# RWKV attention and two expert layers: x2 loads on ScalarE's queue, norm steps placed anew, norm transfers a step later, decay comparison beside the tables

## The chip, the cores and the metric

The kernel runs on one core of a Trainium2 chip. The metric is the device time of one execution in microseconds. Engines are called TensorE (PE in the rows), VectorE (DVE), ScalarE (ACT), GpSimd (POOL) and SyncE (SP, which here only issues transfers).

## The reference, cut to what matters

```python
# attention: B, H, S, D = 4, 8, 768, 48
for t in range(S):
    cur = einsum('bhd,bhe->bhde', u * k[t], v[t])
    y[t] = einsum('bhd,bhde->bhe', r[t], state + cur)
    state = w * state + einsum('bhd,bhe->bhde', k[t], v[t])
# first expert layer: 3072 tokens, 384 -> 768 -> 384
h = maximum(maximum(x @ w1, x @ w2), x @ w3);  x = h @ w_out
# second expert layer: 384 -> 1536 -> 384
xn = x / sqrt(mean(x * x) + 1e-6) * rms_g
g = xn @ w_gate;  val = xn @ w_val
out = (g * sigmoid(g) * val) @ w_out
```

All arrays are float32.

## The kernel before

**Order.** The whole body is one stream written by hand: each engine executes its instructions in the order in which the Python code emits them, and so do the transfer queues of SP and of GpSimd. An instruction that waits holds back all that its engine was given after it. Semaphores are put in by the framework from reads and writes of tiles; a tile of a pool with `bufs=n` takes the place of the tile n before it with the same tag and waits until that one has been read.

**Attention.** Tokens are cut into 24 chunks of 128 (six positions by four batches). `tables()` builds powers of the decay `w` (clamped to 0.7 to 1.1 in `wcl`) by repeated products on VectorE. `decay_flag()` compares `w` with its clamped value (`ok`), sums the comparison with a one-column matmul (`psok`) and makes an integer of it (`nok`); a slow path at the end of the program runs if a decay was clamped. The matmul's bank comes from the pool `psx`, four banks in turn, shared with `pa` (scores), `py` (outputs) and `pkv` (states).

**Units.** The list `UNITS` groups chunks: two of two chunks, five of four. In unit u the main loop runs 18 slots `a_l1` of the first expert layer (f = 0..5, w = 0..2; nine matmuls each into a bank of `psm`, four banks in turn; w = 0 is copied by ScalarE, w = 1, 2 are joined by VectorE's maximum) and, but in the first unit, six slots `a_out`. Between slots, in places set by `LEAD`, it puts the attention steps of the next unit. The flag is taken in unit 1 after slot 8. Products are made of three matmuls on high and low halves (`mm3`, lines 73 to 76), for which ScalarE makes the high half and VectorE or GpSimd subtracts for the low half.

**The last unit** (u = L) has no attention left. After its slot 0 it issues the loads of the first two x2 tiles (output of the first expert layer, kept in DRAM), then the loads of the second expert's weights (`ws_raw`, tiles `gv`, and `wo_raw`, tiles `wof`), all through SP. Between its slots two generators are advanced: `es` (`norm_steps(0)`, then `form_steps(0)`) and `wg` (splitting of weights into high and low halves on ScalarE and GpSimd). The step count of `es` per slot is line 700.

**Norm steps** (lines 546 to 596) for a pair p of x2 tiles, with a yield as a border between steps: 1 to 6 square on ScalarE and add on GpSimd; 7 to 9 and 10 to 12 cast, subtract and sum over partitions with a matmul by ones (`ss`), each closed by a small write to DRAM (`msd`); then a load that spreads the means over partitions (`m`), two idle steps; step 16 the inverse root's start value and two Newton rounds on VectorE, step 17 two more rounds, the write of the roots (`rsd`) and two broadcast loads into `sq`; three idle steps; 21 to 26 scale x2 (line 593). **Form steps** (lines 606 to 631) make four sums and differences, then nine splits; the last three splits wait for slot 18 because they take the place of the unit's own input.

**Second expert.** For each of three pairs p it runs 12 slices f; in each, products `pa`, `pb`, `pc`, `pd`, `px` of the formed inputs with the slice's weights, then the output matmuls. `back(n)`, four times in a slice, advances the weight work (`split_steps`, in pair 0: two splits, then the loads for later slices through SP) and, from slice 2 on, one step of the next pair's norm.

Of the kernel before, what the change touches and what calls it, by code (L numbers as in the profile page):

```python
# [9 lines left out]
F32 = mybir.dt.float32  # L10
# [4 lines left out]
ALU = mybir.AluOpType  # L15
# [22 lines left out]
NP = H // 2  # L38
# [9 lines left out]
def rwkv_moe_kernel(ctx, tc, rkT, rkv, wd, ub, cst, rg, w1p, wo1p, w2p, out):  # L48
    nc = tc.nc
    act, dve, pool, pe, sync = nc.scalar, nc.vector, nc.gpsimd, nc.tensor, nc.sync  # L50
# [8 lines left out]
    tp = sT.enter_context(tc.tile_pool(name="att", bufs=1, side="right"))  # L59
# [121 lines left out]
    qk = tp.tile([96, 2, NP, 128], F32, name="qk")  # L181
    kt = tp.tile([128, DM], F32, name="kt")
    w128 = tp.tile([96, NP], F32, name="w128")
    Tst = [tp.tile([96, NP, 96], F32, name=f"T{b}") for b in range(B)]

    raw_t, tm_t, loads = {}, {}, []
# [16 lines left out]
    def tables():  # L203
        p = ap_.tile([96, NP, 65], F32, tag="h1h", name="ptab")
        pool.memset(p[:, :, 0:1], 1.0)
        dve.tensor_scalar(out=wcl, in0=wsb, scalar1=0.7, scalar2=1.1, op0=ALU.max, op1=ALU.min)
        dve.tensor_copy(p[:, :, 1:2], wcl.unsqueeze(2))
        n = 1
        while n < 64:
            dve.tensor_tensor(out=p[:, :, n + 1:2 * n + 1], in0=p[:, :, 1:n + 1],  # L210
                              in1=p[:, :, n:n + 1].to_broadcast([96, NP, n]), op=ALU.mult)
            n *= 2
        dve.reciprocal(qk[:, 1, :, 64:128], p[:, :, 1:65])
        act.copy(qk[:, 0, :, 64:128], p[:, :, 0:64])
        act.copy(qk[:, 1, :, 0:64], p[:, :, 63::-1])
        act.copy(qk[:, 0, :, 0:64], qk[:, 1, :, 127:63:-1])
        return p
# [13 lines left out]

    def decay_flag():

        ok = tp.tile([96, NP], F32, name="ok")
        dve.tensor_tensor(out=ok, in0=wsb, in1=wcl, op=ALU.is_equal)
        ps = psx.tile([1, NP], F32, tag="x", name="psok")
        pe.matmul(ps, r32(ones[0:96, 0:1]), ok, start=True, stop=True)
        n = cp.tile([1, 1], F32, name="nok")
        dve.tensor_reduce(out=n, in_=ps, op=ALU.add, axis=mybir.AxisListType.X)
        flag = cp.tile([1, 1], mybir.dt.int32, name="okflag")  # L240
        dve.tensor_copy(flag, n)
        return flag
# [219 lines left out]
    with tc.manual_schedule():  # L462
# [83 lines left out]
        def norm_steps(p):  # L546

            br = sB["r"]
            us = (2 * p, 2 * p + 1)
            x = [x2s.pop(u) for u in us]  # L550
            sq = [br.tile([128, 3, 512], F32, tag="sq", bufs=2, name=f"sq{u}") for u in us]
            for j in range(2):
                for k in range(3):
                    act.activation(sq[j][:, k], x[j][:, k], AF.Square)  # L554
                    if k:
                        pool.tensor_tensor(out=sq[j][:, 0], in0=sq[j][:, 0], in1=sq[j][:, k], op=ALU.add)  # L556
                    yield
            for j in range(2):
                sr = br.tile([128, 2, 512], F32R, tag="sr", name=f"sr{us[j]}")
                act.copy(sr[:, 0], sq[j][:, 0])  # L560
                yield
                dve.tensor_tensor(out=sr[:, 1], in0=sq[j][:, 0], in1=r32(sr[:, 0]), op=ALU.subtract)
                yield
                ps = psx.tile([128, 512], F32, tag="x", name=f"ss{us[j]}") if p == 0 else PX[3]
                pe.matmul(ps, ones, sr[:, 0], start=True, stop=False)
                pe.matmul(ps, ones, sr[:, 1], start=False, stop=True)
                act.copy(sq[j][0:1, 1], ps[0:1])
                sync.dma_start(msd[p, j:j + 1], sq[j][0:1, 1])
                yield

            m, y, t = (br.tile([128, 8], F32, tag=f"n{n}", name=f"n{n}{p}") for n in range(3))
            sync.dma_start(m, msd[p].rearrange("j (a b) -> (j a) b", b=8))
            for _ in range(3):
                yield
            dve.tensor_scalar(out=m, in0=m, scalar1=1.0 / DM, scalar2=1e-6, op0=ALU.mult, op1=ALU.add)
            dve.tensor_scalar(out=y.bitcast(U32), in0=m.bitcast(U32), scalar1=1, scalar2=0x7fffffff,
                              op0=ALU.logical_shift_right, op1=ALU.bitwise_xor)
            dve.tensor_scalar(out=y, in0=y, scalar1=1.8352577e-20, scalar2=None, op0=ALU.mult)
            dve.tensor_scalar(out=m, in0=m, scalar1=-0.5, scalar2=None, op0=ALU.mult)
            for n in range(4):  # L580
                if n == 2:
                    yield
                dve.tensor_tensor(out=t, in0=y, in1=m, op=ALU.mult)
                dve.tensor_tensor(out=t, in0=t, in1=y, op=ALU.mult)
                dve.scalar_tensor_tensor(out=y, in0=t, scalar=1.5, in1=y, op0=ALU.add, op1=ALU.mult)
            sync.dma_start(rsd[p].rearrange("j (a b) -> (j a) b", b=8), y)
            for j in range(2):
                sync.dma_start(sq[j][:, 2], rsd[p, j].partition_broadcast(128))
            for _ in range(4):
                yield  # L590
            for j in range(2):
                for k in range(3):
                    dve.scalar_tensor_tensor(out=x[j][:, k], in0=x[j][:, k], scalar=rg_sb[:, k:k + 1],
                                             in1=sq[j][:, 2], op0=ALU.mult, op1=ALU.mult)
                    yield
                xr[us[j]] = x[j]

        def x2_load(u):
            x2s[u] = sB["r"].tile([128, 3, 512], F32, tag="x2", bufs=2, name=f"x2_{u}")
            sync.dma_start(x2s[u], x2d[u])  # L600

        def split(h, lo, x, lo_eng):
            act.copy(h, x)
# [30 lines left out]
        for u in range(len(UNITS)):  # L634
# [9 lines left out]
            for n, sl in enumerate(slots):  # L644
                held = later[:]
                later.clear()
                sl()
                for fn in held:
                    fn()
                want = min(len(todo), -(-len(todo) * (n + 1) // (len(slots) - LEAD[min(u, 1)])))  # L650
                while done < want:
                    todo[done]()
                    done += 1
                    load_next()
                if u == 1 and n == 8:
                    flag = decay_flag()
                elif u == 3 and n == 0:
                    nok = nc.values_load(flag, min_val=0, max_val=DM)
                if u < 2:
                    if tick_n[0] < NJA + 1:  # L660
                        tick(U0T[n] if u == 0 else 1)
                elif 2 <= u < L:
                    if n % 8 in (0, 3, 6):
                        tick()
                elif u == L:
                    if n == 0:
                        for v in range(2):
                            x2_load(v)
                        for f in range(2):
                            ws_raw(f)  # L670
                        for f in range(3):
                            wo_raw(f)

                        def early():
                            yield from norm_steps(0)
                            yield from form_steps(0)

                        def weights():
                            ws_tile(0)
                            for hf in range(2):  # L680
                                ws_split(0, hf, pool)
                                yield
                            ws_raw(2)
                            wo_tile(0)
                            for f in range(2):
                                wo_split(f, pool)
                                yield
                            ws_tile(1)
                            for hf in range(2):
                                ws_split(1, hf, pool)  # L690
                                yield
                            ws_raw(3)
                            ws_tile(2)
                            for hf in range(2):
                                ws_split(2, hf, pool)
                                yield

                        es, wg = early(), weights()
                    if n >= 1:
                        for _ in range(3 if n < 4 or n == 11 else 2):  # L700
                            if n >= 18 or form_left[0] > 3:
                                next(es, None)
                    if n >= 5 and n % 2:
                        next(wg, None)
# [336 lines left out]
```

## Time and profile before

| | us |
|---|---|
| median of 3 runs | 901.02 (900.37 to 901.37) |
| profiled execution | 904.7 |
| its span | 903.0 |
| TensorE busy | 864.4 (96%) |
| VectorE busy | 535.1 (59%) |
| ScalarE busy | 417.8 (46%) |
| GpSimd busy | 254.8 (28%) |
| mean granted TensorE clock | 0.972 |

The span is the time from the first to the last instruction in the trace; the profiled execution is longer than the runs without a profile. Attention and the first units take the time to 408.50 us, the last unit to 468.46, the second expert the rest. A busy share is a mean over these stages.

### The profile page before, as it was taken

The page shows a single profiled execution, that of the slowest core. Times are in us where ns is not written, and L with a number is a line of the kernel's source. Part 1 is how long each engine was busy: PE and PEld are TensorE (multiplying, and loading weights), DVE is VectorE, ACT ScalarE, POOL GpSimd, SP SyncE. Part 2 cuts the span into 40 slices and gives each one's busy share as a digit, 9 for nine tenths or more (in the row PEclk, how much of TensorE's full clock was granted, in tenths as well). Part 3 has the DMA queues.
Part 4 walks back from the last instruction along what each step waited for, and adds up shares of the span by engine and source line. Part 5 has one row for each costly group of instructions (what it writes and reads, how often), then busy time and mean ns, then how long its engine had stood idle before and what let it go on. Part 6 is the DMA issues. An engine that isn't in the chain of part 4 may idle for free.

```text
span 903.0 us, 11986 instructions
## 1 busy us (share of the span) xinstructions
PE 864.4 (96%) x4340; PEld 729.4 (81%) x4340; DVE 535.1 (59%) x831; ACT 417.8 (46%) x795; POOL 254.8 (28%) x219
## 2 busy tenths in 40 slices
PE   7789799999999999998999999999999999999996
PEld 6679798888888888886777787888878888888885
DVE  6899646986986885862655555372445373342342
ACT  3777423444444543413266655464544454444441
POOL 3686742443453441302355634000200000000000
PEclk8689899999999999998999999999999999999998
DMA  6655434466466556415357544064433053333001
GB/s 215 207 183 166 134 111 131 134 169 209 140 171 192 153 166 209 142 61 199 102 183 272 218 165 183 1 244 158 155 108 128 1 209 114 116 125 137 1 36 38
DMA packets 52319, 130.61 MB, mean 145 GB/s; under 512 B 7318, under 2 KB 23958, under 8 KB 47644
## 3 DMA queue, kind: packets, MB, share of 16 engines
q1 hardware_dynamic: 50524, 115.61, 39.9%
q0 software_dynamic: 1728, 14.16, 3.8%
q8 instruction: 36, 0.59, 0.3%
q14 instruction: 31, 0.25, 0.1%
HBM read 93.93 MB, written 33.84 MB: 141 GB/s over the span
## 4 chain that ended last, share of the span: by engine, by line
PE 83%; DVE 8%; issue 2%; ACT 2%; POOL 1%; DMA 1%; SPq 0%; DVEq 0%; ACTq 0%; POOLq 0%
PE pl L74 6%; PE pl L76 6%; PE pl L75 6%; PE po L75 5%; PE po L76 5%; PE po L74 5%; PE py L355 4%; PE pa L74 4%; PE pa L76 4%; PE pa L75 4%; PE px L74 3%; PE px L75 3%; PE px L76 3%; PE pb L74 3%; PE pb L76 3%; PE pb L75 3%
## 5 line engine op out<-in xcount | busy, mean ns | idle before, releaser
L74 PE MATMUL pl<-x,w_a 128*128 128x512 f32 (+1 forms) x378 | 145.5, 385 | 8.1 <-DVE c L439 5.1
L76 PE MATMUL pl<-x,w_a 128*128 128x512 f32 (+1 forms) x378 | 139.2, 368 | 0.6 <-POOL w_a L131 0.6
L75 PE MATMUL pl<-x,w_a 128*128 128x512 f32 (+1 forms) x378 | 139.6, 369 | 0.0
L815 DVE TENSOR_TENSOR v<-pb,es 128x512 f32<-128x512 f32 x36 | 24.9, 692 | 167.2 <-PE pb L76 167.2
L74 PEld LDWEIGHTS pl<-x,w_a 128*128 128x128 f32 x378 | 74.5, 197 | 19.2 <-DVE c L439 5.9
L76 PEld LDWEIGHTS pl<-x,w_a 128*128 128x128 f32 x378 | 74.3, 197 | 12.0 <-POOL w_a L131 0.8
L75 PEld LDWEIGHTS pl<-x,w_a 128*128 128x128 f32 x378 | 74.6, 197 | 9.6 <-DVE x L371 0.3
L439 DVE TENSOR_TENSOR c<-pl,c 128x512 f32<-128x512 f32 (+1 forms) x84 | 50.8, 605 | 33.7 <-PE pl L76 31.2
L288 POOL TENSOR_SCALAR_AFFINE_SELECT Dg<-a 128x1024 f32<-128x1024 f32 x24 | 28.8, 1202 | 129.9 <-DVE a L285 118.4
L355 PE MATMUL py<-Dg,tm 128*96 128x128 f32 x368 | 56.3, 278 | 5.1 <-DVE Dg L308 4.8
L724 ACT CAST hb<-si 128x512 fp32r<-128x512 f32 x36 | 22.3, 620 | 79.0 <-DVE si L818 79.0
L263 ACT ACTIVATE rh<-raw,csb 96x512 fp32r<-96x512 f32 (+1 forms) x48 | 32.1, 715 | 55.9 <-DVE raw L253 51.7
L441 ACT CAST h1h<-c 128x512 fp32r<-128x512 f32 (+1 forms) x36 | 19.8, 549 | 78.3 <-DVE c L439 78.3
L355 PEld LDWEIGHTS py<-Dg,tm 128*96 128x96 f32 x368 | 46.4, 167 | 6.5 <-DVE Dg L308 5.8
L122 DVE SCALAR_TENSOR_TENSOR wf<-wf,wraw 128x384 uint32<-128x384 uint32 x60 | 50.8, 848 | 0.0
L308 DVE COPY_PREDICATED Dg<-csb,pa 128x512 f32<-128x512 uint32 x48 | 35.2, 734 | 23.3 <-PE pa L76 16.9
L519 POOL TENSOR_TENSOR ws<-gv,ws 128x576 fp32r<-128x576 f32 x24 | 35.6, 1486 | 46.5 <-ACT ws L518 46.5
L117 DVE SCALAR_TENSOR_TENSOR wraw<-wf,wraw 128x384 uint32<-128x384 uint32 x60 | 48.2, 803 | 0.0
L556 POOL TENSOR_TENSOR sq<-sq 128x512 f32<-128x512 f32 x12 | 16.5, 1380 | 107.6 <-ACT sq L554 107.4
L74 PE MATMUL pc<-z,ws 128*128 128x512 f32 x108 | 42.5, 394 | 2.2 <-ACT pd L810 2.2
L277 POOL TENSOR_TENSOR ru<-tm,usb 128x384 f32<-128x384 f32 x23 | 28.7, 1246 | 54.9 <-DMA tm<-in_rkv 54.9
L74 PE MATMUL pb<-f,ws 128*128 128x512 f32 x108 | 42.5, 394 | 0.1
(187 smaller groups left out, 2296.7 us busy)
## 6 DMA issues: line engine op xcount, KB each, us to landing
ws<-w2s SPq DMA_DIRECT2D x24, 1152.0 KB, 5.2
wraw<-in_w2p SPq DMA_DIRECT2D x36, 384.0 KB, 3.6
w2s<-ws POOLq DMA_DIRECT2D x12, 1152.0 KB, 5.1
raw<-in_rkT SPq DMA_DIRECT2D x24, 384.0 KB, 4.4
tm<-in_rkv SPq DMA_DIRECT2D x24, 384.0 KB, 4.1
tm<-in_rkv SPq DMA_DIRECT2D x24, 288.0 KB, 3.1
wraw<-in_w1p SPq DMA_DIRECT2D x18, 384.0 KB, 3.7
w2d<-wf SPq DMA_DIRECT2D x36, 192.0 KB, 3.7
```

Source lines behind the costliest of these rows:

```text
L74: pe.matmul(o, lh, rh, start=start, stop=False, **kw)
L75: pe.matmul(o, lh, rl, start=False, stop=False, **kw)
L76: pe.matmul(o, ll, rh, start=False, stop=stop, **kw)
L117: dve.scalar_tensor_tensor(out=clow(n), in0=cw[n].bitcast(U32), scalar=3, in1=clow(n), op0=ALU.logical_shift_left, op1=ALU.bitwise_or)
L122: dve.scalar_tensor_tensor(out=wu, in0=wu, scalar=0x80000000, in1=clow(n), op0=ALU.bitwise_and, op1=ALU.bitwise_or)
L263: act.activation(rh[:, :, j], raw[:, 0], AF.Copy, scale=m01[0:96, j:j + 1])
L277: eng.tensor_tensor(out=ru, in0=tm[:, 0:DM], in1=usb, op=ALU.mult)
L288: pool.affine_select(out=Dg, in_=a8.unsqueeze(2).to_broadcast([128, H, 128]), pattern=[[0, H], [1, 128]], channel_multiplier=-1, base=0, c ...
L308: dve.copy_predicated(out=dg, mask=cmask.unsqueeze(1).to_broadcast([128, 4, 128]), data=pa.rearrange("p q j t -> p (q j) t"))
L355: pe.matmul(py[0:96, pr], tm[:, VO + 144 * pr + 48 * j:VO + 144 * pr + 48 * j + 96], s["Dg"][:, 2 * pr + j], start=(c == 0 and j == 0), st ...
L439: dve.tensor_tensor(out=c1[:, :n], in0=p[:, :n], in1=c1[:, :n], op=ALU.max)
L519: lo_eng.tensor_tensor(out=t[:, 1, sl], in0=r[:, sl], in1=r32(t[:, 0, sl]), op=ALU.subtract)
```

## The change

The comparison `ok` moves from `decay_flag` into `tables`. In the last unit the first two x2 loads are issued by ScalarE, the later four stay with SP. The `es` steps per slot become: none after slots 0 and 1, three after slots 2 and 3, one after slots 4 to 14 but two after slot 6, three from slot 15 on (before: three after slots 1 to 3 and 11, two after the others). In `norm_steps` of pairs 1 and 2 one idle step each is put ahead of the load of the means, ahead of the write of the roots and between that write and the broadcasts.

```diff
@@ rwkv_moe_kernel
+    ok = tp.tile([96, NP], F32, name="ok")
@@ tables
         dve.tensor_scalar(out=wcl, in0=wsb, scalar1=0.7, scalar2=1.1, op0=ALU.max, op1=ALU.min)
+        dve.tensor_tensor(out=ok, in0=wsb, in1=wcl, op=ALU.is_equal)
@@ decay_flag
-        ok = tp.tile([96, NP], F32, name="ok")
-        dve.tensor_tensor(out=ok, in0=wsb, in1=wcl, op=ALU.is_equal)
         ps = psx.tile([1, NP], F32, tag="x", name="psok")
@@ norm_steps
+            if p:
+                yield
             sync.dma_start(m, msd[p].rearrange("j (a b) -> (j a) b", b=8))
...
+            if p:
+                yield
             sync.dma_start(rsd[p].rearrange("j (a b) -> (j a) b", b=8), y)
+            if p:
+                yield
             for j in range(2):
                 sync.dma_start(sq[j][:, 2], rsd[p, j].partition_broadcast(128))
@@ x2_load
-            sync.dma_start(x2s[u], x2d[u])
+            (sync if u > 1 else act).dma_start(x2s[u], x2d[u])
@@ last unit
-                    if n >= 1:
-                        for _ in range(3 if n < 4 or n == 11 else 2):
+                    if n >= 2:
+                        for _ in range(1 if 4 <= n < 15 and n != 6 else 2 if n == 6 else 3):
                             if n >= 18 or form_left[0] > 3:
                                 next(es, None)
```

## Rows read from the trace of the kernel before

**Rows 1.** The page, chain that ended last: shares of the span by engine.

```profile
PE 83%; DVE 8%; issue 2%; ACT 2%; POOL 1%; DMA 1%; SPq 0%; DVEq 0%; ACTq 0%; POOLq 0%
```

**Rows 2.** TensorE's waits: waiting line <- releaser: us in total, times, longest us.

```profile
PE psok L237 <- DVE ok L235: 3.8, 1, 3.8
PE ss L565 <- ACT sr L560: 2.6, 1, 2.6
PE pc L74 <- ACT pd L810: 2.2, 2, 2.0
```

**Rows 3.** Timeline, TensorE, decay flag: start us, us, line, out<-in, [idle <-releaser].

```profile
102.71 0.19 PE L237 MATMUL psok<-ok,ones 96*1 96x4 f32 x2 [3.84 <-DVE ok L235]
109.90 1.03 PE L306 MATMUL pa<-rh,raw 96*128 96x256 f32 x4
```

**Rows 4.** Timeline, VectorE, the same stretch.

```profile
100.87 0.55 DVE L285 TENSOR_REDUCE a<-ru 128x8 f32<-128x384 f32 x1 [2.31 <-POOL ru L278]
101.67 0.99 DVE L235 TENSOR_TENSOR ok<-wsb,wcl 96x4 f32<-96x4 f32 x1
109.40 0.54 DVE L377 TENSOR_TENSOR x<-py,x 96x384 fp32r<-96x384 f32 x1
```

**Rows 5.** Windows: stretch, us, busy of each engine (count), PEclk, DMA share, GB/s.

```profile
102.71:109.90 7.19, 7.19 (x33) 6.80 (x34) 3.32 (x7) 1.02 (x4) 6.20 (x6) 0.55 0.02 6
409.70:420.30 10.60, 7.62 (x33) 5.76 (x31) 3.24 (x4) 5.43 (x10) 4.44 (x4) 0.98 1.00 350
421.10:426.64 5.54, 5.54 (x15) 4.34 (x13) 1.29 (x2) 1.09 (x2) 0.48 (x1) 0.50 0.00 0
545.43:549.64 4.21, 4.21 (x11) 3.34 (x12) 3.30 (x4) 2.15 (x4) 3.36 (x4) 0.59 0.38 149
```

**Rows 6.** Timeline, VectorE, opening.

```profile
10.67 0.56 DVE L277 TENSOR_TENSOR ru<-tm,usb 128x384 f32<-128x384 f32 x1 [3.25 <-DMA usb<-in_ub]
```

**Rows 7.** Timeline, TensorE, last unit and start of the second expert.

```profile
408.50 0.39 PE L74 MATMUL pl<-x,w_a 128*128 128x512 f32 x1
416.44 0.39 PE L76 MATMUL pl<-x,w_a 128*128 128x512 f32 x1
421.10 0.63 PE L74 MATMUL pl<-x,w_a 128*128 128x512 f32 x1
452.02 0.50 PE L74 MATMUL pl<-x,w_a 128*128 128x512 f32 x1 [1.11 <-DVE c L439]
470.02 0.50 PE L74 MATMUL pb<-f,ws 128*128 128x512 f32 x1
```

**Rows 8.** Timeline, ScalarE, last unit.

```profile
410.79 0.59 ACT L436 COPY c<-pl 128x512 f32<-128x512 f32 x1 [1.50 <-PE pl L76]
414.42 1.68 ACT L554 ACTIVATE sq<-x 128x512 f32<-128x512 f32 x3 [3.04 <-DMA x<-x2d]
```

**Rows 9.** Timeline, VectorE, last unit.

```profile
442.17 0.75 DVE L593 SCALAR_TENSOR_TENSOR x<-x,rg_sb,sq 128x512 f32<-128x512 f32 x1 [3.88 <-DMA sq<-rsd]
448.12 1.92 DVE L442 TENSOR_TENSOR h<-c,h 128x512 fp32r<-128x512 f32 x1
464.05 3.95 DVE L604 TENSOR_TENSOR f<-y,f 128x512 fp32r<-128x512 f32 x3 [0.40 <-ACT f L603]
```

**Rows 10.** Timeline, SP's queue, last unit.

```profile
409.74 0.89 SPq L600 DMA_DIRECT2D x<-x2d  x2
436.34 0.34 SPq L586 DMA_DIRECT2D rsd<-n  x1
```

**Rows 11.** Transfers issued: out<-in, queue, count, KB each, median us to landing.

```profile
x<-x2d SPq DMA_DIRECT2D x6, 768.0 KB, 7.2
```

**Rows 12.** Timeline, SP's queue, second expert, first pair.

```profile
533.77 0.32 SPq L586 DMA_DIRECT2D rsd<-n  x1
536.06 0.38 SPq L510 DMA_DIRECT2D gv<-w2d  x1
```

**Rows 13.** Timeline, ScalarE, second expert, first pair.

```profile
543.72 0.67 ACT L518 CAST ws<-gv 128x576 fp32r<-128x576 f32 x1 [2.98 <-DMA gv<-w2d]
```

## The prediction

> **What bounds the kernel now.** I read the chain that ended last first: 83% of the span is TensorE at work, 8% VectorE and 2% ScalarE [rows 1]. So only time in which TensorE waits, or runs at the lower of its two clock levels, can be won. The waits of TensorE's own queue come next [rows 2]; the three that this change touches are the decay flag's matmul (3.8 us), the first norm sum of the last unit (2.6 us) and one `pc` matmul in the second expert (2.0 us). Then I opened the timeline of each engine around these three places, and the windows behind them for the granted clock. The other long waits of that list lie at the start of the kernel, in code that the change leaves alone.
>
> **Part 1, the decay comparison.** Before, the comparison of four numbers per partition stood on VectorE at 101.67 and took 0.99 us, behind a reduction that had waited 2.31 us for GpSimd [rows 4]. The flag's matmul waited for it from 98.87 to 102.71 [rows 3], and 33 matmuls behind it ran at a granted clock of 0.55 until 109.90 [rows 5]. With the comparison beside the tables its result is there long before, and the tile that had the matmul's bank is read by then, so it runs at 98.9. The 33 matmuls take 7.19 x 0.55 = 4.0 us at the full level, until 102.9. Then comes what is late next: the matmul at 109.90 takes the bank of the last `py` tile, which is free when VectorE's subtraction at 109.40 has read it [rows 3, 4]. VectorE does 3.32 us of work between 102.71 and 109.90 [rows 5]; none of it waits for the comparison, so counted from 101.67 it is done at 105.0. TensorE is thus 4.9 us ahead at this point, with a new wait of 2.1 us in it. A wait of 2.0 us at 543.4 was followed by 4.21 us at a clock of 0.59 [rows 5], a loss of 4.21 x 0.41 = 1.7 us; the loss after the 3.8 us wait was 7.19 x 0.45 = 3.2 us. So the part is worth 4.9 us with no drop and 1.7 us with the larger one; I take 3.2, since the nearest wait in length is the 2.0 us one. In the opening the comparison adds at most its 0.99 us to VectorE, which there waits 3.25 us for a load [rows 6]: nothing; without that cover it would be 0 to 0.99 us.
>
> **Part 2, the last unit.** 35 matmuls of 512 columns lie between 408.50 and 416.44, 0.227 us each [rows 7]; a slot of nine is 2.04 us. 24 slots, four norm sums and six matmuls of the second expert make 226 matmuls or 51.3 us, so that `pb` could start at 459.8. It starts at 470.02 [rows 7]: 10.2 us are lost. 4.0 us of it are the gap from 416.44 to 421.10 less three matmuls, some 2.7 us are 5.54 us at a clock of 0.50 behind it [rows 5], and the rest are waits for a late VectorE, the largest 1.11 us at 452.02 [rows 7].
>
> The first gap goes as follows. ScalarE waits 3.04 us for the first x2 tile, squares, GpSimd adds, ScalarE casts, VectorE subtracts, and TensorE stands after slot 3 for it [rows 8]. Now slots 0 and 1 give no norm step, and the sum stands after slot 6, at 422.8 instead of 416.7. The loads are issued by ScalarE behind its copy of slot 0, at about 411.4 instead of 409.74 [rows 8, 10]; two issues cost ScalarE about what they cost SP, 0.89 us, and it is idle there for 3.04 us, so that price is nothing (0 to 0.89 without the cover). On SP the weight loads move up by the same 0.89 us, ahead of the x2 loads. The transfer engines were busy without a break from 409.70 to 420.30 [rows 5], so the order decides who is late: the first x2 tile took 4.6 us when it went first, and 7.2 us is the median over all six such loads [rows 11]. I put its landing at 416 to 419.5 and the second's at 418 to 420.5, the end of that busy stretch. Queued behind the waiting square on ScalarE are the copies and casts of slots 2 and 3; TensorE needs their banks only from slot 7, at 423.3. From the second landing to the second sum matmul there are three squares (1.68 us, [rows 8]), a cast and a subtraction of about 0.7 to 0.9 us each: 3.3 us. So a landing up to 419.5 costs nothing, one at 420.5 a microsecond. I take 0.7.
>
> Then the chain through DRAM. Before, the inverse roots left at 436.34 and their broadcast let VectorE go on at 442.17, after a wait of 3.88 us: 5.83 us [rows 9, 10]. Now step 17, which issues them, stands after slot 13, which ends at 438.0 with the two sums counted; a maximum and six small operations later it is 439.9, and the broadcast is there at 445.8. The first scaling stands after slot 15 (442.1), so VectorE waits about as long as before. Queued behind it is the maximum of slot 16, whose bank TensorE wants at slot 20 (450.3): covered. Left for VectorE from 445.8 are six scalings, two maxima, one low part, four sums and six low parts, 19 operations of 128x512. At 0.70 us (the row of 442.17 less its overlap) they end at 459.1, at the 1.32 us of the three at 464.05 they end at 470.9 [rows 9]; the one at 448.12 took 1.92. GpSimd has five subtractions to do beside them; with five of the 19 at the longer time that is 3.1 us on the lower end: 462. The matmul `pb` needs the last but one of them and waits until about 461.5, 1.7 us more than the floor. The part gives 10.2 - 0.7 - 1.7 = 7.8, less 0.4 for a share of low clock behind the new wait: 7.4 us. Its bounds are 10.2 (no wait) and 2.3 (the second rival below).
>
> The row shows that VectorE's operations with two inputs from SBUF last 0.75 us at one place and 1.32 to 1.92 at another [rows 9]. By the Trainium skill (SBUF — State Buffer, "Who interferes with whom") such an operation and one of GpSimd that reads SBUF exclude each other for a whole instruction. By that rule, with all seven low parts of this stretch blocked for the 0.62 us between the rows, the part would give 10.2 - 0.7 - 3.1 = 6.4 us, and by the short row alone 9.5.
>
> **Part 3, the transfers of the later norms.** In the second expert's first pass the queue of SP held the write of the inverse roots, issued at 533.77 when VectorE had them, and the weight load behind it went out at 536.06 [rows 12]. ScalarE waited 2.98 us for that load [rows 13], and TensorE behind it 2.0 us [rows 2], then 1.7 us at the lower clock as worked out above. With the steps moved, that weight load (three transfers of slice 10, one of the output weights) stands ahead of the root's write on SP, and its buffer is free when GpSimd's subtraction of slice 8, two slices back, has ended. The wait goes whole: 3.7 us, between 0 (the load is still late) and 3.7. Past it on SP are now the root's write and two broadcasts, whose first reader comes three steps later, on a VectorE that has room; the next weight load follows them by less than it does now. In the other two norms TensorE shows no such wait, so they give nothing.
>
> **The sum.** 3.2 + 7.4 + 3.7 = 14.3 us. The profiled execution took 904.7 us (span 903.0 and 1.7 around it), 3.7 more than the median of the runs; less 14.3 it is 890.4, and the median 901.0 becomes 886.7.
>
> **Rivals.** First: the x2 loads share the transfer engines packet by packet and both land at about 421; TensorE waits 1.5 to 2 us for the first sum and then runs slow as after 421.10, some 3 us less in part 2. For it speaks the busy stretch [rows 5], against it that the stretch ends at 420.3. Time 889.7. The Trainium skill (DMA: Bandwidth & Descriptors, "Issuing engines are not separate DMA queues") says that transfers from any engine interleave on the same sixteen engines and that a second issuer saves issue time alone; by that rule this rival is the case, and the 7.2 us median agrees with it.
>
> Second: VectorE bounds the end of the unit. Before, its work after the broadcast ran from 442.17 to 468.0; six operations (4.2 us) now lie ahead of it, which leaves 21.6, from 445.8 to 467.4. `pb` starts at 466.0, 4.0 us early, less 1.7 at the low clock: part 2 gives 2.3, and the time is 891.8. For it speaks the chain of contended rows [rows 9], against it that VectorE also waited within that stretch.
>
> Third: the change does not do what it says; each wait comes back at the next late bank or load, and only one of parts 1 and 3 is left: 897 to 901.
>
> Fourth, on the other side: ScalarE's queue itself. It works in order, and no row shows it issuing a load. Past 419.5 each microsecond by which the second x2 tile lands later is one of TensorE, and ScalarE's copies behind it hold the banks from slot 7 on. From a landing at 435.6 the 14.3 us and the 1.8 of the bound are used up; at 440 the time is 886.7 + 20.5 - 0.7 = 906.5. Against it: all bytes of that stretch had moved by 420.3.
>
> **Chances.** Forecast 0.57, first rival 0.17, second 0.13, third 0.08, fourth 0.05. About 0.2% (1.8 us) is what a measurement of this kernel can tell from no change: half of the third case lies within it, so faster 0.91, same 0.04, slower 0.05. The range goes from all upper bounds (4.9 + 10.2 + 3.7 = 18.8, or 882.2) past both first rivals to a loss of two parts: 882.0 to 895.5.
>
> **What would show it.** Right: no wait of TensorE at the flag's matmul and a shorter one at the `pa` matmul after slot 11; the first norm sum after slot 6 with less than 1.5 us of wait; a clock of 1.0 through slots 4 to 10; the first scaling still waiting 3 to 4 us for the broadcast; no `pc` wait in the ninth or tenth slice of the first pass. Wrong: squares starting later than 421, `pb` more than 4 us behind its floor, or weight loads still behind the root's write.

## The result, and the profile after

| | before | after |
|---|---|---|
| median | 901.19 us (900.37 to 902.55) | 889.56 us (888.08 to 890.51) |
| profiled execution | 904.7 us | 889.44 us |
| its span | 903.0 us | 887.7 us |

The ratio of the medians is 0.9879 [0.9859, 0.99], 11.6 us less. The two profiled executions differ by 15.3 us; why they differ by more is taken up with the second trace of the kernel before. 886.7 us was forecast, 2.9 us less than the median; the change won 11.6 of the 14.3 us forecast. That the sum came this near is partly luck: one of its three terms was too small and another much too large.

The chain that ended last, after: shares of the span by engine, against [rows 1]:

```profile
PE 85%; DVE 7%; DMA 3%; ACT 2%; issue 2%; POOL 1%; SPq 0%; ACTq 0%; DVEq 0%; POOLq 0%
```

TensorE's waits after (waiting line <- releaser: us in total, times, longest us), against [rows 2]: the flag (`psok`) and `pc` are gone, the norm sum (`ss`) has shrunk, and a wait at `px`, the second expert's first product of the second formed set, is new.

```profile
PE px L75 <- DVE f L610: 2.6, 1, 2.6
...
PE ss L566 <- DVE sr L562: 0.6, 1, 0.6
...
PE ss L565 <- ACT sr L560: 0.4, 1, 0.4
```

**The flag.** TensorE's timeline after (start us, us, line, out<-in), against [rows 3]; VectorE's, against [rows 4], stands behind it:

```profile
97.15 0.19 PE L237 MATMUL psok<-ok,ones 96*1 96x4 f32 x2
...
101.46 1.03 PE L306 MATMUL pa<-rh,raw 96*128 96x256 f32 x4
```

The window between these two rows (columns as in [rows 5]; the clock is the third figure from the end):

```profile
97.15:101.46 4.31, 4.31 (x35) 4.16 (x35) 1.53 (x5) 2.16 (x7) 3.51 (x5) 1.00 0.86 251
```

VectorE:

```profile
100.04 0.14 DVE L239 TENSOR_REDUCE nok<-psok 1x1 f32<-1x4 f32 x1
...
103.98 0.53 DVE L377 TENSOR_TENSOR x<-py,x 96x384 fp32r<-96x384 f32 x1
```

The `pa` matmul runs at 101.46 without a wait, 2.5 us before VectorE's L377 has even begun to read the `py` tile. By the order of the program, four banks in turn, it should take that tile's bank; it doesn't. Which bank it takes instead isn't shown; of the reads ahead of it, VectorE's of the flag's own bank at 100.04 would fit.

**The last unit.** ScalarE after (against [rows 8]): its queue issues the two loads at 403.58, and the squares begin 7.7 and 10.0 us later.

```profile
403.58 0.86 ACTq L606 DMA_DIRECT2D x<-x2d  x2
...
411.25 1.67 ACT L554 ACTIVATE sq<-x 128x512 f32<-128x512 f32 x3 [2.54 <-DMA x<-x2d]
...
413.57 1.67 ACT L554 ACTIVATE sq<-x 128x512 f32<-128x512 f32 x3 [0.17 <-DMA x<-x2d]
```

SP and VectorE after (against [rows 9, 10]): the roots' write, the first scaling, and the last operations ahead of `px`.

```profile
436.19 0.32 SPq L590 DMA_DIRECT2D rsd<-n  x1
```

```profile
430.67 0.99 DVE L577 TENSOR_SCALAR n<-n 128x8 f32<-128x8 f32 x1
...
432.18 1.29 DVE L585 TENSOR_TENSOR n<-n,n 128x8 f32<-128x8 f32 x1
...
440.71 0.75 DVE L599 SCALAR_TENSOR_TENSOR x<-x,rg_sb,sq 128x512 f32<-128x512 f32 x1 [2.57 <-DMA sq<-rsd]
...
447.81 1.80 DVE L620 TENSOR_TENSOR y<-x,y 128x512 f32<-128x512 f32 x1
449.54 1.78 DVE L622 TENSOR_TENSOR x<-x,x 128x512 f32<-128x512 f32 x1
452.01 4.53 DVE L610 TENSOR_TENSOR z<-x,z 128x512 fp32r<-128x512 f32 x3 [0.69 <-ACT z L609]
456.46 1.88 DVE L610 TENSOR_TENSOR f<-y,f 128x512 fp32r<-128x512 f32 x3
```

The other small operations of this step take 0.17 us each. GpSimd beside them: its operation of 432.02 ends where VectorE's long one of 432.18 ends (433.45 and 433.47), and one of 430.52 (1.11 us) where that of 430.67 ends (431.63 and 431.66):

```profile
432.02 1.43 POOL L519 TENSOR_TENSOR ws<-gv,ws 128x576 fp32r<-128x576 f32 x1 [0.38 <-ACT ws L518]
```

TensorE after, against [rows 7]: the unit starts at 401.05, and `pb` stands 56.77 us behind (before 61.52; the floor was 51.3). The window behind `px` (columns as in [rows 5]) has the lower clock.

```profile
401.05 0.39 PE L74 MATMUL pl<-x,w_a 128*128 128x512 f32 x1
...
457.19 0.50 PE L75 MATMUL px<-f,ws 128*128 128x512 f32 x1 [2.62 <-DVE f L610]
...
457.82 0.63 PE L74 MATMUL pb<-f,ws 128*128 128x512 f32 x1
```

```profile
457.70:461.10 3.40, 3.40 (x9) 2.65 (x9) 0.64 (x2) 2.27 (x4) 0.46 (x1) 0.50 1.04 347
```

**The transfers.** SP's queue after, against [rows 12]: a set of weight loads now goes out at 514.09, ahead of the roots' write; before, none stood between 522.04 and that write.

```profile
514.09 0.32 SPq L510 DMA_DIRECT2D gv<-w2d  x1
...
522.06 0.32 SPq L590 DMA_DIRECT2D rsd<-n  x1
```

### The profile page after: what moved, and what is told of

Read it like the earlier page. It is cut to its first block, busy times and chain, and to the rows that moved or that the text cites. A ratio compares the mean times of both kernels' runs of the same rounds, so it can differ in the third digit from the quotient of the medians.

```text
span 887.7 us, 11979 instructions
## 1 busy us (share of the span) xinstructions
PE 857.4 (97%) x4340; PEld 724.8 (82%) x4340; DVE 534.2 (60%) x831; ACT 417.2 (47%) x795; POOL 259.7 (29%) x219
## 4 chain that ended last, share of the span: by engine, by line
PE 85%; DVE 7%; DMA 3%; ACT 2%; issue 2%; POOL 1%; SPq 0%; ACTq 0%; DVEq 0%; POOLq 0%
PE pl L74 7%; PE pl L76 7%; PE pl L75 7%; PE po L74 5%; PE po L76 5%; PE po L75 5%; PE py L355 4%; PE pa L74 4%; PE pa L75 4%; PE pa L76 4%; PE px L75 4%; PE px L74 4%; PE px L76 4%; PE pb L74 3%; PE pb L76 3%; PE pb L75 3%
## 5 line engine op out<-in xcount | busy, mean ns | idle before, releaser
L74 PE MATMUL pl<-x,w_a 128*128 128x512 f32 (+1 forms) x378 | 142.9, 378 | 6.4 <-DVE c L439 3.4
L76 PE MATMUL pl<-x,w_a 128*128 128x512 f32 (+1 forms) x378 | 137.0, 363 | 0.6 <-POOL w_a L131 0.6
L75 PE MATMUL pl<-x,w_a 128*128 128x512 f32 (+1 forms) x378 | 137.1, 363 | 0.0
L74 PEld LDWEIGHTS pl<-x,w_a 128*128 128x128 f32 x378 | 72.4, 191 | 16.6 <-DVE c L439 3.8
L76 PEld LDWEIGHTS pl<-x,w_a 128*128 128x128 f32 x378 | 72.3, 191 | 12.0 <-POOL w_a L131 0.8
L75 PEld LDWEIGHTS pl<-x,w_a 128*128 128x128 f32 x378 | 72.5, 192 | 9.3 <-DVE x L371 0.3
L74 PE MATMUL pa<-f,ws 128*128 128x512 f32 x108 | 42.6, 394 | 0.0
```

Of the source, the lines that this page charges most:

```text
L74: pe.matmul(o, lh, rh, start=start, stop=False, **kw)
L75: pe.matmul(o, lh, rl, start=False, stop=False, **kw)
L76: pe.matmul(o, ll, rh, start=False, stop=stop, **kw)
```

## The experiments

The kernel before ran again beside each group of runs: its median was 898.82 us for the first four sections, 899.69 for the next four, 901.06 for the three after those and 901.16 for the last. The groups ran on different chips, so runs of different groups are compared by their ratios to it; a gain in us is one less the ratio, times that median.

### The kernel before once more

No edit; a second trace.

> The kernel before, profiled once more. Its profiled execution took 904.7 us against a median of 901.2, while that of the changed kernel stood at its own median; the two profiles differ by 15.3 us, the medians by 11.6. Theory: the three waits of before (3.8 us at the flag, 2.6 at the first norm sum, 2.0 at pc) are in every execution, and the first profile had about 3.5 us of extra waiting elsewhere, so this one has a span near 900 with all three waits in it. Rival: one of the three waits comes and goes, and it is missing here while the span is near 899.

One run of 898.7 us, span 896.9. The three waits are there again:

```profile
PE psok L237 <- DVE ok L235: 3.8, 1, 3.8
PE pc L74 <- ACT pd L810: 2.3, 2, 2.0
PE ss L565 <- ACT sr L560: 2.2, 1, 2.2
```

But the clock behind them isn't the same. Behind `pc` the window has 1.00, where [rows 5] had 0.59; behind the norm sum 0.74, where it had 0.50.

```profile
541.82:545.82 4.00, 4.00 (x18) 3.31 (x19) 3.31 (x3) 2.17 (x4) 3.51 (x4) 1.00 0.29 109
419.34:424.88 5.54, 5.54 (x19) 4.47 (x20) 1.29 (x2) 1.09 (x2) 1.08 (x1) 0.74 0.00 0
```

So the waits belong to the kernel, but how long the lower clock lasts behind one differs from execution to execution. The first trace lost 5.54 x 0.24 = 1.3 us more than this one behind the norm sum, and 4.21 x 0.41 = 1.7 us more behind `pc`. These 3.0 us are half of the 6.1 us by which the spans of the two traces differ, and as much as most of the 3.7 us between 15.3 and 11.6. That they are the reason for those 3.7 us is argued, not shown: the runs without a profile left no trace. The last unit differs too: from its first matmul to `pb` it took 61.52 us in the first trace and 59.38 in this one.

### The flag alone

```diff
@@ tables
+        dve.tensor_tensor(out=ok, in0=wsb, in1=wcl, op=ALU.is_equal)
@@ decay_flag
-        dve.tensor_tensor(out=ok, in0=wsb, in1=wcl, op=ALU.is_equal)
```

> The kernel before with the decay comparison beside the tables, nothing else. Theory (from the two profiles): TensorE is 6.8 us earlier after this point, 3.8 us of waiting and 3.0 us of half clock behind it, and keeps it to the end: about 894.5. Rival, as predicted: the scores' matmul two slots later takes up a part as a new wait for the bank of the last output tile, 3.2 us in all: about 898. Second rival: the lead is lost in the last unit, where VectorE bounds: within 1 us of before.

893.99 us (891.41 to 896.89), ratio 0.9937 [0.9915, 0.996]: 5.7 us, by the interval 3.6 to 7.6. After the flag its trace shows no new wait of TensorE over 0.12 us until the norm sum:

```profile
98.69 0.19 PE L237 MATMUL psok<-ok,ones 96*1 96x4 f32 x2
...
413.14 0.50 PE L565 MATMUL ss<-sr,ones 128*128 128x512 f32 x1 [2.26 <-ACT sr L560]
```

The new bank wait that the prediction put behind the flag isn't there, and nothing is lost again in the last unit, whose waits are as before.

### The last unit alone

```diff
@@ x2_load
-            sync.dma_start(x2s[u], x2d[u])
+            (sync if u > 1 else act).dma_start(x2s[u], x2d[u])
@@ last unit
-                    if n >= 1:
-                        for _ in range(3 if n < 4 or n == 11 else 2):
+                    if n >= 2:
+                        for _ in range(1 if 4 <= n < 15 and n != 6 else 2 if n == 6 else 3):
```

> The kernel before with ScalarE's x2 loads and the new step counts of the last unit, nothing else. Theory (from the two profiles): the last unit up to the first pc of the second expert shortens by 3.4 us, since the px matmul waits 2.6 us for VectorE and 3.4 us run at half clock: about 897.5. Rival, as predicted: 7.4 us, about 894. Second rival: without the earlier parts its clock does not fall and it gives 5 us, about 896.

896.72 us (894.53 to 900.03), ratio 0.9974 [0.9955, 0.9993]: 2.3 us, by the interval 0.6 to 4.0. The wait at `px` comes with this part, at the same length as with all three. Here the window behind it has the full clock, as the second rival had it, though not its 5 us; `pb` stands 57.06 us behind the unit's start:

```profile
463.26 0.50 PE L75 MATMUL px<-f,ws 128*128 128x512 f32 x1 [2.61 <-DVE f L604]
```

```profile
463.26:467.26 4.00, 4.00 (x17) 3.30 (x18) 1.15 (x2) 3.04 (x5) 1.23 (x1) 1.00 1.03 350
```

### The transfers alone

```diff
@@ norm_steps
+            if p:
+                yield
...
             sync.dma_start(rsd[p].rearrange("j (a b) -> (j a) b", b=8), y)
+            if p:
+                yield
```

(and the same ahead of the load of the means)

> The kernel before with the idle steps in the later norms, nothing else. Theory: no pc matmul waits for a late weight load in the tenth slice, 2.0 us of waiting and 1.7 us of half clock go: about 897.4. Rival: that wait was in the first profile alone; no change, 901 within 1 us.

894.68 us (893.73 to 897.99), ratio 0.9958 [0.994, 0.9976]: 3.8 us, by the interval 2.2 to 5.4. The 2.0 us wait at `pc` is gone. The product of the three ratios, 0.9937 x 0.9974 x 0.9958 = 0.9869, is within the interval of the whole (0.9879): within the noise the parts add up.

### The x2 loads back on SP

```diff
-            (sync if u > 1 else act).dma_start(x2s[u], x2d[u])
+            sync.dma_start(x2s[u], x2d[u])
```

> The changed kernel with all x2 loads on SP again. Theory: on ScalarE's queue the two loads share the transfer engines with the weight loads and land 7.6 and 9.5 us after their issue; first on SP they land within about 4.6 and 6.5 us of an issue 1.3 us earlier, and the 1.05 us that TensorE waits for the first norm sum go: 0.5 to 1 us faster than the changed kernel, less than the clock can hide, so the waits of the profile decide. Rival: the ScalarE queue is what removes the first wait of the last unit; on SP the wait at the first norm sum grows above 2 us.

887.84 us (887.12 to 888.45), ratio 0.987 [0.9848, 0.9891]. TensorE doesn't wait for the norm sums at all, and `px` waits as long as before:

```profile
415.90 0.39 PE L565 MATMUL ss<-sr,ones 128*128 128x512 f32 x1
416.40 0.50 PE L566 MATMUL ss<-sr,ones 128*128 128x512 f32 x1
...
456.44 0.79 PE L75 MATMUL px<-f,ws 128*128 128x512 f32 x1 [2.62 <-DVE f L610]
```

ScalarE's queue is not what shortened the first norm wait; the later place of the steps is. The queue costs about 1 us of waits at the sums, and `pb` stands 0.9 us earlier without it (55.85 us behind the unit's start); the times don't tell the two kernels apart.

### The weight splits earlier

```diff
-                    if n >= 5 and n % 2:
+                    if 5 <= n <= 12:
                         next(wg, None)
```

> The changed kernel with the eight weight-split steps of the last unit after each of slots 5 to 12 instead of every other slot from 5 to 19. Theory: the px matmul waits 2.6 us because GpSimd's weight splits lie beside VectorE's operations behind the broadcast and lengthen them from 0.7 to 1.5 or 1.8 us each; without them the wait falls below 1 us and the time by 2 to 5 us, to about 886. Rival: the broadcast's landing bounds; the operations stay as long or the wait stays above 2 us.

888.01 us (887.57 to 889.0), ratio 0.9874 [0.9852, 0.9896]: no gain. The idea was to take GpSimd's weight subtractions away from VectorE's late operations. The three `z` low parts do fall from 4.53 to 2.23 us, but GpSimd's own low parts of the formed set still lie beside the two operations ahead, and the first scaling came 1.3 us later, 40.97 us behind the unit's start instead of 39.66:

```profile
442.76 0.75 DVE L599 SCALAR_TENSOR_TENSOR x<-x,rg_sb,sq 128x512 f32<-128x512 f32 x1 [3.67 <-DMA sq<-rsd]
...
449.86 1.67 DVE L620 TENSOR_TENSOR y<-x,y 128x512 f32<-128x512 f32 x1
451.45 1.78 DVE L622 TENSOR_TENSOR x<-x,x 128x512 f32<-128x512 f32 x1
453.92 2.23 DVE L610 TENSOR_TENSOR z<-x,z 128x512 fp32r<-128x512 f32 x3 [0.69 <-ACT z L609]
```

### The casts of the norm sums earlier

```diff
-                        for _ in range(1 if 4 <= n < 15 and n != 6 else 2 if n == 6 else 3):
+                        for _ in range(3 if n < 4 or n > 14 else 2 if n in (6, 10, 14) else 1):
```

> The changed kernel with norm steps 15 to 17 one slot earlier, so that the roots are written after slot 12 instead of 13. Rival of the theory in the run before: the landing of the broadcast bounds; 2 us earlier it takes 2 us from the px wait, which falls to about 0.6 us, and the time by 2 to 4 us, to about 887. Theory: the operations behind it stay lengthened by GpSimd, VectorE waits as long at the first scaling, and the px wait falls by less than 1.5 us.

886.34 us (884.14 to 887.23), ratio 0.9851 [0.9828, 0.9874]. The roots leave 32.3 us behind the start of the unit instead of 35.1, the wait at `px` falls to 0.59 us, and part of it moves to the output matmul of the unit:

```profile
449.92 0.50 PE L75 MATMUL po<-h,w_o 128*128 128x512 f32 x1 [1.14 <-DVE h L442]
456.37 0.50 PE L75 MATMUL px<-f,ws 128*128 128x512 f32 x1 [0.59 <-DVE f L610]
```

So the chain ahead of the broadcast was late, and by it VectorE. Of the 2.8 us that it is earlier, 1.9 reach `pb` (54.83 us behind the start instead of 56.77).

### All three of these edits

> The three edits together: x2 loads on SP, splits early, roots one slot earlier. Theory: no wait of TensorE above 0.5 us between the start of the last unit and the second expert, pb starts 52 us after the unit's start instead of 56.8, and the half-clock stretch behind it goes: 883 to 886. Rival: splitting early crowds ScalarE and GpSimd between slots 5 and 12 and the second norm sum comes late; not faster than the changed kernel.

888.13 us (887.32 to 888.81), ratio 0.9873 [0.9851, 0.9894]: a miss. The roots leave early, but the broadcast is issued 3.4 us after them instead of 1.4, and TensorE waits 3.05 us at the output matmul:

```profile
434.66 0.32 SPq L590 DMA_DIRECT2D rsd<-n  x1
438.07 0.80 SPq L594 DMA_DIRECT2D sq<-rsd  x2
```

```profile
451.28 0.50 PE L75 MATMUL po<-h,w_o 128*128 128x512 f32 x1 [3.05 <-DVE h L442]
```

SP issues nothing in between, so the broadcast waits for the roots' write itself (4 KB, 1.4 us from issue to landing at the median). With early splits that took 2.2 us (the kernel with these alone) and 3.4 us. In these two windows the transfer engines were 53% and 75% busy; in the windows of 1.4 us, of the changed kernel and of the one with earlier casts, 6%. GpSimd's write of split weights (1152 KB) went out 2.7 and 1.4 us ahead of the roots, where in the changed kernel it goes out 4.1 us behind them. So the early splits put a large write beside the small one; that this is what holds it up is argued from these four windows. The window here, the DMA share being the last figure but one:

```profile
434.66:438.07 3.41, 3.41 (x16) 2.82 (x15) 1.96 (x3) 1.11 (x2) 0.00 (x0) 1.00 0.75 304
```

### Loads on SP and casts earlier

> The changed kernel with two edits that each stood alone before: the first two x2 loads go out through SP again, and the casts of the norm sums come earlier (three norm steps after slots 2 and 3, two after slots 6, 10 and 14). Theory (what is left of the loss in the last unit is the landing of the broadcast, a chain x2 load, squares, sums, roots, broadcast; each part that shortens it counts): the loads by SP made the first norm sum free of waits (about 1.0 us less in the trace) and the early casts brought the first scaling 1.1 us forward, so the two together give the early casts' 886.3 less 0.5 to 1.0: 885.3 to 885.9; the first scaling at most 31.5 us before pb. Rival (VectorE's lengthened operations behind the broadcast bound it whatever comes earlier): 886.3 or a little more, with the px wait at about 1 us.

886.96 us (886.29 to 888.09), ratio 0.9848 [0.9824, 0.9871], the same as with the casts alone. The theory that each part of the chain still counts falls; what is left lies on VectorE behind the broadcast.

### And no GpSimd subtractions beside VectorE

The kernel before this, and

```diff
-                    split(h[:, k], lo[:, k], x[:, k], pool if p == 0 and n == 0 else dve)
+                    split(h[:, k], lo[:, k], x[:, k], dve)
```

> The kernel of e8_sp_cast with the three low parts of the first formed set taken by VectorE instead of GpSimd. Theory (GpSimd's subtractions of 128x512 lengthen VectorE's two-input operations that run beside them from about 0.7 us to 1.8 us): the sums and differences that lie beside them fall from 1.7 to 1.9 us to 0.7 to 0.8 each, two to three of them, 2 to 3 us less, against three low parts of 0.7 us more for VectorE (2.1 us): the wait at px changes by less than 1 us and the time by less than 1 us from e8_sp_cast. Rival (they are long by themselves, for instance for what they read): they stay at 1.7 to 1.9 us, VectorE is 2 us later and the wait of px grows by about 2 us; time 2 us over e8_sp_cast.

884.52 us (883.18 to 885.43), ratio 0.9815 [0.9791, 0.9838], 2.4 us faster than without this edit on the same chip. VectorE's rows and GpSimd's low parts beside them without it, then VectorE's with it:

```profile
447.63 1.75 DVE L442 TENSOR_TENSOR h<-c,h 128x512 fp32r<-128x512 f32 x1
449.31 1.78 DVE L622 TENSOR_TENSOR x<-x,x 128x512 f32<-128x512 f32 x1
```

```profile
447.13 5.12 POOL L610 TENSOR_TENSOR f<-x,f 128x512 fp32r<-128x512 f32 x3
```

```profile
448.43 0.68 DVE L442 TENSOR_TENSOR h<-c,h 128x512 fp32r<-128x512 f32 x1
449.03 0.68 DVE L622 TENSOR_TENSOR x<-x,x 128x512 f32<-128x512 f32 x1
449.63 1.88 DVE L610 TENSOR_TENSOR f<-x,f 128x512 fp32r<-128x512 f32 x3
```

The two operations lose their 1.1 us each, and the three low parts cost VectorE 1.88 us where they cost GpSimd 5.12. The mechanism was as expected; the time fell by more than the theory's 1 us. The waits show 1.2 us less at the output matmul, 0.4 at `px` and 0.3 at `pb`. It beats both kernels: 5.2 us below the changed one, run on the same chip (889.68, next).

### The changed kernel once more

> The changed kernel itself once more, for a comparison on one chip with e8_sp_cast and e9_low_dve and for a second trace of it. Theory (the profiled executions of the kernel before and of this one differed by more than the medians because the stretch at half clock behind one and the same wait differs between executions): the same waits of TensorE as in the first trace, within 0.3 us each (px about 2.6, first norm sum 0.4 and 0.6), no wait at the flag and none at pc, but a stretch at half clock behind px of another length (none, 3.4 or 6.8 us); median 888 to 890. Rival (the stretch belongs to the wait's length): 3.4 us again.

889.68 us (888.79 to 890.09), ratio 0.9874 [0.9851, 0.9897]. The wait at `px` is 2.62 us again, and so is a stretch at the lower clock behind it:

```profile
458.26 0.64 PE L75 MATMUL px<-f,ws 128*128 128x512 f32 x1 [2.62 <-DVE f L610]
```

```profile
458.26:461.66 3.40, 3.40 (x8) 2.64 (x9) 1.15 (x2) 1.55 (x3) 0.00 (x0) 0.53 1.09 378
```

So the rival's 3.4 us came, not another length. But with the last unit alone the same wait (2.61 us) left the clock at 1.00, so the length of the wait doesn't decide it either. What decides stays open.

### The comparison written into `wcl`

The fastest kernel, and

```diff
-    ok = tp.tile([96, NP], F32, name="ok")
...
-        dve.tensor_tensor(out=ok, in0=wsb, in1=wcl, op=ALU.is_equal)
         dve.tensor_copy(p[:, :, 1:2], wcl.unsqueeze(2))
+        dve.tensor_tensor(out=wcl, in0=wsb, in1=wcl, op=ALU.is_equal)
```

> The kernel of e9_low_dve with the comparison written into the tile wcl itself, behind its last use, so that no tile ok is made among the attention's tiles and these stand where they stood in the kernel before. In every trace with the comparison beside the tables the stretch from the flag's matmul to the first matmul of the last unit takes 303.84 to 303.90 us, each attention position 15.13 where the kernel before took 15.09; the longer position began with the moved tile. Theory (the place of the attention's tiles in SBUF makes it): 15.09 a position, 302.8 to 303.0 us from the flag's matmul to the last unit, and 1.0 us less in the time, about 883.5. Rival (it goes with something else that the moved comparison changes, such as the order in which the banks of scores and outputs come free): 303.84 to 303.90 and 15.13 again, time as e9_low_dve, 884.5.

884.07 us (883.07 to 885.6), ratio 0.9816 [0.9788, 0.9844]: no difference. From the flag to the last unit it is 403.33 - 99.47 = 303.86 us, as in all kernels with the moved comparison.

```profile
99.47 0.19 PE L236 MATMUL psok<-wcl,ones 96*1 96x4 f32 x2
...
403.33 0.39 PE L74 MATMUL pl<-x,w_a 128*128 128x512 f32 x1
```

An attention position (one chunk) takes 15.13 us here too. So the place of the tiles made ahead of the flag is not the cause of the longer positions. The tiles first made behind the flag (`rl`, `kh`, `kl`) had `ok` made ahead of them in the kernel before and have not here, so their place was not brought back; that theirs is the cause is unlikely, but not ruled out.

## Why the prediction was right, and where it wasn't

| part | forecast us | alone on the chip us |
|---|---|---|
| 1, the flag | 3.2 | 5.7 (3.6 to 7.6) |
| 2, the last unit | 7.4 | 2.3 (0.6 to 4.0) |
| 3, the transfers | 3.7 | 3.8 (2.2 to 5.4) |
| sum | 14.3 | 11.8 |

**Part 1** won more than forecast; whether it won more than its upper bound of 4.9 the interval leaves open. The wait at the flag went, and behind it 35 matmul records took 4.31 us at a granted clock of 1.00, as worked out. The step that failed is "the matmul at 109.90 takes the bank of the last `py` tile": `pa` ran before that tile was read. So there was no 2.1 us wait and no drop of the clock behind it. At this `pa` TensorE was 109.90 - 101.46 = 8.4 us ahead, 1.7 of which it had already at the flag (102.71 - 3.84 = 98.87 against 97.15, by chance of the opening), which leaves 6.7: 3.84 us of waiting and 2.9 of the lower clock. Up to the last unit 1.0 us of it was given back: 408.50 - 102.71 = 305.8 us from the flag's matmul before, 303.9 after, so that 1.9 is left of the lower clock's loss, and 3.84 + 1.9 = 5.7. Most attention positions take 15.13 us after and 15.09 before, which is part of that 1.0; why stays open.

**Part 2** won a third of the forecast. The second rival's price was the same 2.3, but as 4.0 less 1.7 at the lower clock, and the trace of this part alone has no lower clock there: the equal figures are partly chance. The place of the first sum was right: ScalarE's loads landed by 413.5, 12.5 us behind the unit's start where the forecast had 9.5 to 12, and the sums waited 0.43 + 0.62 = 1.05 us where 0.7 was set. The term that was mis-sized is the wait ahead of `pb`, 1.7 us "less 0.4 for a share of low clock". Counted from the start of the unit, the roots left at 35.1 us where the forecast had 31.4 (439.9 - 408.5). "A maximum and six small operations later" left out that TensorE reaches the end of slot 13 some 2 us later, and that step 16's ten small operations, two of them lengthened to 0.99 and 1.29 us, hold back slot 13's maximum on VectorE. The trip through DRAM was shorter, 4.5 us instead of 5.83, so the first scaling was 39.7 us behind the start instead of 37.3: 2.4 late. Behind it VectorE took 16.4 us to `px` instead of 15.7. That is 3.1 us: `px` at 56.14 instead of the 53.0 that the forecast had for `pb`, which itself came at 56.77. Then, in this trace, came 3.40 us at 0.50 behind it, 1.7 us, where 0.4 was set.

`pb` 5.5 us behind its floor is past the 4 us that the prediction named as a sign of being wrong, and the first scaling waited 2.57 us where it named 3 to 4. Part of what is missing is the base. The forecast took `pb` from 61.52 us behind the unit's start to 53.0; the second trace of the kernel before has 59.38, and the trace of this part alone 57.06, which is 2.3 us less. Of the 5.1 us by which the part fell short, 2.1 are thus the base and 4.1 a later `pb`, less the 1.1 us that the forecast had taken off for the sums and the clock.

The casts made earlier took back half of the lateness, and then the contention on VectorE was what was left; GpSimd's three subtractions moved away took most of that. So the second rival's mechanism, a VectorE that bounds the end of the unit, was nearer than the forecast's.

The prediction allowed 0.62 us for each operation of VectorE beside GpSimd. The rows show 1.1: 1.75 and 1.78 us fall to 0.68 when GpSimd's subtractions go. GpSimd's low parts take 1.7 us each there (5.12 for three). The flag's own comparison of four elements a partition, 101.67 to 102.66 [rows 4], ended with a GpSimd instruction that ended at 102.65:

```profile
101.56 1.09 POOL L288 TENSOR_SCALAR_AFFINE_SELECT Dg<-a 128x1024 f32<-128x1024 f32 x1 [0.72 <-DVE a L285]
```

By the Trainium skill (SBUF — State Buffer, "Who interferes with whom") VectorE's instructions with two inputs in SBUF and GpSimd's that read SBUF hold a shared pair of ports for a whole instruction. These rows agree: the wait is what is left of GpSimd's instruction. The rows after show the same of an operation with one input, L577 at 430.67: 0.99 us instead of 0.17, up to the end of GpSimd's.

**The rivals.** The first rival had the later landing right: counted from the unit's start its 421 is 12.5 us, and the second tile was there at 12.5, the first at 10.2. The two loads took 7.6 and 9.5 us beside SP's weight loads, where the first took 4.6 on SP, ahead of them. What failed in it is the price: TensorE waited 1.05 us in all for the sums, not 1.5 to 2 for the first, and the clock stayed at 1.00 up to 457.7. All three waits went or shrank (third), and TensorE waited for none of ScalarE's copies behind the loads (fourth).

**Part 3** went as worked out: the weight loads of one slice stand ahead of the roots' write, and the wait went whole. Its size is less sure than the table looks: 1.7 of the 3.7 us are lower clock behind `pc`, which of four traces with this wait only the first has.

The base also matters: the sum was taken off one execution with 6.8 us of lower clock behind the norm sum and 3.4 behind `pc`. The second trace of the same kernel had half of the first and none of the second, so what a wait costs beyond its own length is a mean over executions that one trace can't show. Over all traces, the lower clock behind the norm sum's wait (2.2 to 2.6 us) lasted 6.8 us twice and 3.4 twice; behind that of `pc` (1.9 to 2.0) 3.4 us once and three times none; behind that of `px` (2.6) 3.4 us three times and once none.

## What to carry to other kernels

When a wait is to be removed, price its own length first, up to the next thing that is late, and the clock behind it as a range from nothing to what one trace shows; two traces of the kernel before would have shown that here. Where VectorE is on the path, list what GpSimd executes beside it: an operation there, however small, can wait for GpSimd's instruction to end, so work moved back from GpSimd can cost VectorE less than it costs beside it (1.88 us for three low parts here, against twice 1.1). Before naming a late bank as the next wait, look for a matmul of the same pool that ran before the supposed reader had finished.

## What the runs showed of the hardware that was not expected

A comparison of 96x4 elements took 0.99 us, because it lasted as long as the GpSimd instruction beside it; it was the last link of a chain, behind a reduction that had itself waited 2.31 us for GpSimd [rows 4], that held up TensorE by 3.84 us. Two loads of 768 KB through ScalarE's queue beside SP's weight loads landed 7.6 and 9.5 us after issue. A write of 4 KB let its reader go 1.4 us after its issue while the transfer engines were 6% busy, after 2.2 us at 53% and 3.4 at 75%. Behind one and the same wait of 2.6 us (`px`) the lower clock lasted 3.4 us or not at all, behind the norm sum's 6.8 us or 3.4.
